# Decay sums of the first head pair on their own, masks made beside the first MLP layer, and a new order of the opening loads

## The chip, the cores and the metric

The kernel runs on one core of one Trainium2 chip. The metric is device time in microseconds (us). Times in the text count from the start of the profiled span unless they are durations. Engine names follow the profile: PE (matrix engine), DVE (vector), ACT (scalar), POOL (GpSimd) and SP (the engine that only issues transfers).

## The reference

The reference is an attention with a decay bias, whose output goes through a two-layer MLP with a hard-swish:

```python
batch, n_heads, seq, head_dim = (8, 8, 576, 64)
scores = q @ k.T / sqrt(64)                    # per head
cum = cumsum(max(s, 0))                        # per head, along the sequence
scores = where(causal, -1e9, scores + min(-(cum[i] - cum[j]), 0))
attn = softmax(scores); x = attn @ v           # (8, 8, 576, 64) -> (4608, 512)
h = x @ w_in                                   # w_in (512, 2048)
g = h * clip(h + 3, 0, 6) / 6
out = g @ w_out                                # w_out (2048, 512), out (4608, 512)
```

All inputs and the output are float32.

## The kernel before

**Units of work.** The 64 heads are taken in 32 pairs; pairs 4b to 4b+3 make up batch b. For a pair, q and k come in as 9 tiles of 128 rows (two heads of 576 rows), are cast to half size and turned, so that the head dimension lies on the partitions (`qT`, `kT`, both in `qkT`, three slots, pair p in slot p % 3). The decay enters as extra rows below the 64 rows of the head dimension: rows 64 to 67 carry the running sum, split in three half-size parts, and a row of ones. Rows 68 to 127 hold a mask by blocks of ten positions. Scores, exp on ACT, the product with v (`attend`), the division and the turn back into `xT` (`x_transpose`) follow. The MLP works on blocks of 512 tokens: `m1` is layer 1 (16 column groups, each four matmuls, an ACT and a DVE instruction), `m2` layer 2 (16 matmuls and a store for each 128 tokens).

**Order.** The program fixes the order on every engine by hand: each engine takes its instructions one after the other in the order in which the program issues them, with waits on semaphores between the engines. PE's order is fixed too. There are three stretches.

1. *Pairs 0 to 3 (batch 0).* There is no MLP work yet. `first_columns` gets the running sums of the first five pairs by four small matmuls of a scan with 0/1 matrices (`sums`), and writes them as columns 64 to 67 beside the cast q and k (`x0`), so that `turn_first` turns data and decay at once. `cast_first` casts q and k, `scores_half` computes half of a head's scores, with the causal mask added by a matmul of `ident` with `tri`. The mask rows of slot 0 are made on POOL by `select` at the very start (L154), the other slots' by DVE copies (`mask_rows`, L191).
2. *The passage to the MLP.* POOL issues the loads of `w_in` (L488) and `w_out` (L494), sets the ones of the decay rows (`aug_ones`, L194 and L195), and after DVE's `decay_scan` makes the rows (`decay_rows`, L147 to L151). PE meanwhile runs layer 1 of block 0. It turns the decay rows into columns (`decay_columns`, L263), which POOL puts in order (`decay_order`, L279 and L282). POOL casts pair 4 (L774, L301), and PE turns it (L780).
3. *Pairs 4 to 31*, woven with the MLP, and the rest of the MLP. Pairs 4 to 9 get their decay rows through memory (`store_aug`, `load_aug`), later ones as columns of `xb` with a transposing DMA.

**Queues.** Plain loads go through SP in the order of the program. The weights go through POOL's queue, since they are cast on the way. On SP, the store of the decay rows is followed by a `fence`, a small transfer that reads a row of the third quarter of `w_out_sb` and so waits for its load, and only then by the loads of pair 4. The lines of the passage read:

```python
    for c in range(4):
        load_w_out(c)
    aug_ones()
    ...
    decay_rows()
    store_aug(nc.sync)
    nc.sync.dma_start(out=fence_dram, in_=w_out_sb[0:1, 11, 0:32])
    load_pair(FIRST)
```

Of the kernel before, what the change touches and what calls it, by code (L numbers as in the profile page):

```python
# [9 lines left out]
F32 = mybir.dt.float32  # L10
# [6 lines left out]
def kernel(  # L17
# [48 lines left out]
    def pair_of_banks(b):  # L66
# [4 lines left out]
    NG = COLS * W2 // 64  # L71
    g = np.arange(NG)
    sel_np = g[:, None] == g[None, :]
    low_np = (g[:, None] < g[None, :]) & (g[:, None] // 9 == g[None, :] // 9)
    sums_dram = nc.inline_tensor(
        np.ascontiguousarray(
            np.stack([m[:, k::2] for k in range(2) for m in (sel_np, low_np)], axis=1)
        ).astype(np.float32),
        name="sums",
    )  # L80
# [28 lines left out]
    dec = cpool.tile([128, NTR, 4, NP], F16, tag="c_dec")  # L109
# [13 lines left out]
        "p (a t i c) -> p a t i c", a=COLS, t=NTR, i=2  # L123
# [3 lines left out]
    sums = work.tile([NG, 4, NG // 2], F32, tag="sums", bufs=1)  # L127
# [31 lines left out]
    def mask_view(sl, i):  # L159
# [4 lines left out]
    nc.vector.memset(x0[:, :, :, 0, D:D + 3], 1.0)  # L164
    nc.vector.memset(x0[:, :, :, 1, D + 3:D + 4], 1.0)
    both = [[0, 2], [1, SEQ]]
    select(
        mask_view(0, 1), both, 4 * GRAN, -GRAN, -16384.0,
        warm[64:128, 0:1].unsqueeze(1).to_broadcast([64, 2, SEQ]),
    )  # L170
    select(ident, [[1, 128]], 0, -1, 0.0, one[:, 0:1].to_broadcast([128, 128]))
    select(ident, [[-1, 128]], 0, 1, 0.0)

    def key_rows():
        nc.vector.memset(one[:, 1:2], 1.0)
        k_rows = mask_view(0, 0)
        select(
            k_rows, both, 4 * GRAN, -GRAN, 0.0,
            one[64:128, 1:2].unsqueeze(1).to_broadcast([64, 2, SEQ]),
        )  # L180
        select(k_rows, [[0, 2], [-1, SEQ]], -4 * GRAN + GRAN - 1, GRAN, 0.0)
        select(tri, [[1, 128]], 0, -1, -65504.0, warm[:, 0:128])
# [6 lines left out]

    def mask_rows(sl, i):  # L190
        nc.vector.tensor_copy(out=mask_view(sl, i), in_=mask_view(0, i))  # L191
# [81 lines left out]
    def decay_order():  # L273
        dv = dec_f.rearrange("p i (t a h) -> p t i a h", t=NTR, h=2)
        for r0, r1, j0, j1, h in (
            (0, 128, 0, 4, 0), (0, 64, 4, 5, 0), (64, 128, 4, 5, 1), (0, 128, 5, 9, 1)
        ):
            for i in range(3):
                nc.gpsimd.tensor_copy(  # L279
                    out=dec[r0:r1, j0:j1, i, :], in_=dv[r0:r1, j0:j1, i, :, h]  # L280
                )
        nc.gpsimd.tensor_scalar_mul(out=dec[:, :, 3, :], in0=dec[:, :, 0, :], scalar1=-1.0)  # L282

    def cast_columns(p):
        x = xb[:, p % 2]
        nc.gpsimd.tensor_copy(  # L286
            out=x.rearrange("p (i t) c -> p t i c", i=2)[:, :, :, 0:D], in_=qk_f.pop(p)
        )
        nc.gpsimd.tensor_copy(out=x[:, NTR:2 * NTR, D:D + 3], in_=dec[:, :, 0:3, p])
        nc.gpsimd.tensor_copy(out=x[:, 0:NTR, D + 3:D + 4], in_=dec[:, :, 3:4, p])  # L290
# [106 lines left out]
    def scores_half(hd, half):  # L397
        p, hh = hd // 2, hd % 2
        sl = p % NS
        off = hh * SEQ  # L400
        b, p0, parts, masks = HALVES[half]
        S = pair_of_banks(b)
        ops = []
        for kt, lo, hi, c in parts:
            ops.append((
                c, hi - lo, kT[:, sl, off + 128 * kt:off + 128 * (kt + 1)],
                qT[:, sl, off + lo:off + hi],
            ))
        for c, n in masks:
            ops.append((c, n, ident, tri[:, 0:n]))  # L410
        ops.sort(key=lambda o: o[0] // 512)
        for i, (c, n, lhsT, rhs) in enumerate(ops):
            bk = c // 512
            nc.tensor.matmul(  # L414
                out=S[:, c:c + n], lhsT=lhsT, rhs=rhs,
                start=(i == 0 or ops[i - 1][0] // 512 != bk),
                stop=(i == len(ops) - 1 or ops[i + 1][0] // 512 != bk),
            )
        n = max(c + n for c, n, _, _ in ops)
        nc.scalar.activation(  # L420
            out=Pm[:, hd % NS, p0:p0 + n], in_=S[:, 0:n], func=AF.Exp, scale=0.125, bias=0.0
        )
# [38 lines left out]
    def x_transpose(p):  # L461
        b, hp = p // (H // 2), p % (H // 2)
        xs = x_tiles.pop(p)
        if by_dma(p):

            nc.sync.dma_start(
                out=xT[:, hp, b * SEQ:b * SEQ + 640].rearrange("p (t c) -> p t c", c=128),
                in_=xs.rearrange("p t h d -> p (t h d)"),
                transpose=True,
            )  # L470
            return
        pX = f16(PS[:, 4 if p + 1 < FIRST else 2, :], 640) if p < FIRST else f16(bank("S"), 640)
        for qt in range(5):
            nc.tensor.matmul(  # L474
                out=pX[:, qt * 128:(qt + 1) * 128],
                lhsT=xs[:, qt, :, :],
                rhs=ident,
                is_transpose=True,
                start=(qt == 0),
                stop=(qt == 4),  # L480
            )
        nc.vector.tensor_copy(out=xT[:, hp, b * SEQ:(b + 1) * SEQ], in_=pX[:, 0:SEQ])  # L482
# [165 lines left out]
    def second_pair(p, fill):  # L648
# [27 lines left out]
        if first:  # L676
            transpose_group(p + 1, 0)
        if p + 3 < PTD:
            load_aug(p + 3, nc.sync)
# [66 lines left out]
    def first_columns():  # L746
# [6 lines left out]
        key_rows()  # L753
        cT = PS[:, 7, 0:NG // 2]
        for half in range(2):
            o = cT[64 * half:64 * half + 64, :]
            nc.tensor.matmul(
                out=o, lhsT=scan, rhs=sums[:, 2 * half, :], start=True, stop=False
            )
            nc.tensor.matmul(  # L760
                out=o, lhsT=scan[:, 63:64].to_broadcast([NG, 64]), rhs=sums[:, 2 * half + 1, :],
                start=False, stop=True,
            )
        c3 = cT.rearrange("p (a t) -> p a t", a=COLS)
        r3 = rest.rearrange("p (a t) -> p a t", a=COLS)
        hi, mid, lo = (x0[:, :, :, 1, D + j] for j in range(3))
        nc.vector.tensor_copy(out=hi, in_=c3)
        nc.scalar.activation(out=x0[:, :, :, 0, D + 3], in_=hi, func=AF.Copy, scale=-1.0)
# [4 lines left out]
    def cast_first(p, i, t0, t1, copy):  # L773
        copy(out=x0[:, p, t0:t1, i, 0:D], in_=qk_f[p][:, t0:t1, i, :])  # L774

    def turn_first(p, i, t0, t1, b, copy):
        pT = f16(pair_of_banks(b) if (t1 - t0) > 8 else PS[:, b, :], (t1 - t0) * 128)
        for t in range(t0, t1):
            c = (t - t0) * 128
            nc.tensor.matmul(  # L780
                out=pT[0:XW, c:c + 128], lhsT=x0[:, p, t, i, :], rhs=ident,
# [11 lines left out]
    A.dma_start(out=sums, in_=sums_dram.ap())  # L793
    load_part(0, 1, 0, 5, nc.sync)
    load_part(0, 0, 5, 9, nc.sync)
    load_part(0, 1, 5, 9, nc.sync)
    nc.scalar.preload_act_table_set("natural_log_exp_and_others")
    load_qk(1, nc.sync)
    load_v(0, nc.sync)
    load_qk(2, nc.sync)  # L800
    load_v(1, nc.sync)

    keep_warm(6)
    cast_first(0, 0, 0, 5, A.copy)
    cast_first(0, 1, 0, 5, A.copy)
    first_columns()
    keep_warm(2)
    turn_first(0, 0, 0, 5, 4, A.copy)
    turn_first(0, 1, 0, 5, 5, V.tensor_copy)
    cast_first(0, 0, 5, 9, G.tensor_copy)  # L810
    cast_first(0, 1, 5, 9, G.tensor_copy)
    for i in range(2):
        mask_rows(1, i)
    keep_warm(1)
    qk_f.pop(0)

    def cast_pair(p):
        for i in range(2):
            cast_first(p, i, 0, NTR, G.tensor_copy)
        qk_f.pop(p)  # L820

    for hd in range(2 * FIRST):
        p, odd = hd // 2, hd % 2
        scores_half(hd, 0)
        if hd == 0:
            turn_first(0, 0, 5, 9, 6, V.tensor_copy)
            turn_first(0, 1, 5, 9, 7, V.tensor_copy)
        if not odd:
            if p == 0:
                cast_pair(1)  # L830
                more_pads()
            if p == 2:
                for c in range(2):
                    load_w_in(c)
            cast_v(p)
            if p + 1 < FIRST:
                turn_first(p + 1, 0, 0, 9, 4, V.tensor_copy)
            if p == 2:
                for c in range(2, 4):
                    load_w_in(c)  # L840
            if p == 0:
                load_qk(3, nc.sync)
                load_v(2, nc.sync)
            if p == 1:
                load_v(3, nc.sync)
                nc.sync.dma_start(out=s_sb, in_=s.rearrange("b h t -> (b h) t"))
                load_columns()
        elif p + 1 < FIRST:
            turn_first(p + 1, 1, 0, 9, 4, V.tensor_copy)
            if p + 2 < FIRST:  # L850
                cast_pair(p + 2)
        scores_half(hd, 1)
        if hd > 0:
            attend(hd - 1)
        if hd == 1:
            for i in range(2):
                mask_rows(2, i)
        if odd and p > 0:
            x_transpose(p - 1)
# [3 lines left out]
    m1_0 = m1_tasks(0)  # L863
    attend(2 * FIRST - 1)
# [10 lines left out]
    decay_rows()  # L875
    store_aug(nc.sync)
    nc.sync.dma_start(out=fence_dram, in_=w_out_sb[0:1, 11, 0:32])
    load_pair(FIRST)
    for p in range(COLS, COLS + 2):
        load_pair(p)  # L880
        load_aug(p, nc.sync)
    run(m1_0[4:8])
# [9 lines left out]
    for i in range(2):  # L892
        copy_columns(i)
# [50 lines left out]
```

The softmax here doesn't subtract the row's maximum and nothing guards it: scores larger than these inputs give would overflow.

## Time and profile before

| | us |
|---|---|
| three runs | 360.22 to 360.40, median 360.33 |
| the profiled execution's own time | 359.87 |
| its span in the profile | 358.20 |
| PE busy | 349.6 (98%) |
| ACT busy | 208.8 (58%) |
| DVE busy | 182.9 (51%) |
| POOL busy | 153.3 (43%) |
| transfers, mean over the span | 165 GB/s |

The span is the stretch that the profiler covers, 1.67 us less than the execution's own time. Busy time counts what an engine's instructions took; waiting, branching and the issue of transfers are not in it. A row such as "22.19 2.17 POOL L494 ... x4" of the timeline gives start, length, engine, source line and how many instructions were merged; what stands in brackets is the idle time before it and what ended it. "DMA to landing" is the time from a transfer's issue to its completion.

### The profile page before, as it was taken

The numbers are of one execution on the slowest core, as the hardware profiler recorded it, in microseconds if no ns is written. First come the engines' busy times: TensorE is split into PE (matmuls) and PEld (weight loads), VectorE is DVE, ScalarE is ACT, GpSimd is POOL, SyncE is SP. The second block draws the span as 40 slices with busy tenths as digits, with TensorE's granted clock in tenths as the row PEclk, the third lists the DMA queues.
The fourth block names the chain that finished last, engine by engine and source line by source line (L and its number), as shares of the span: only waits on it lengthen the run. The fifth ranks groups of instructions, "written<-read, shape, count | busy, mean of one in ns | idle before, by whom it ended". The sixth has DMA issues, their size and how long they took to land.

```text
span 358.2 us, 7700 instructions
## 1 busy us (share of the span) xinstructions
PE 349.6 (98%) x2860; PEld 204.2 (57%) x2860; DVE 182.9 (51%) x314; ACT 208.8 (58%) x391; POOL 153.3 (43%) x378
## 2 busy tenths in 40 slices
PE   7999999999999999999999999999999999999996
PEld 3875557665655555555555555555555544544444
DVE  3758737766534553455435553545255536544531
ACT  3777437668847774677467755776477614533410
POOL 6694377765654444444444554555543200000000
PEclk9999999999999999999999999999999999999999
DMA  8999999999989999999998999999947110000012
GB/s 180 214 193 214 212 228 223 215 208 203 210 180 229 197 197 221 229 210 185 185 249 172 207 204 211 170 208 211 224 87 116 50 59 30 31 30 29 32 59 88
DMA packets 185312, 59.09 MB, mean 165 GB/s; under 512 B 177576, under 2 KB 180050, under 8 KB 185274
## 3 DMA queue, kind: packets, MB, share of 16 engines
q1 hardware_dynamic: 181681, 54.05, 72.0%
q0 software_dynamic: 2688, 4.19, 6.6%
q8 instruction: 22, 0.36, 0.4%
q10 hardware_dynamic: 905, 0.36, 0.4%
q14 instruction: 16, 0.13, 0.1%
HBM read 37.32 MB, written 9.53 MB: 131 GB/s over the span
## 4 chain that ended last, share of the span: by engine, by line
PE 84%; DVE 4%; ACT 3%; DMA 3%; POOL 3%; issue 1%; SPq 1%; POOLq 0%; ACTq 0%; DVEq 0%
PE PS L506 32%; PE PS L549 32%; PE PS L348 10%; PE PS L436 7%; DMA qkf<-in_k_dram 3%; DVE gT L517 2%; ACT trl L516 2%; DVE qkT L319 1%; ACT Pm L356 1%; PE PS L569 1%; PE PS L474 1%; PE PS L304 1%; POOL gT L774 1%; PE PS L414 1%; SPq L206 1%
## 5 line engine op out<-in xcount | busy, mean ns | idle before, releaser
L517 DVE SCALAR_TENSOR_TENSOR gT<-trl,PS 128x512 f16<-128x512 f32 x144 | 98.2, 687 | 103.0 <-ACT trl L516 102.9
L516 ACT ACTIVATE trl<-PS,bias 128x512 f32<-128x512 f32 x144 | 98.8, 692 | 78.3 <-PE PS L506 76.5
L506 PE MATMUL PS<-xT,w_in 128*128 128x512 f16 x576 | 143.2, 380 | 0.8 <-DVE gT L517 0.7
L549 PE MATMUL PS<-w_out_sb,gT 128*128 128x512 f16 x560 | 138.9, 379 | 0.0
L356 ACT ACTIVATE Pm<-PS 128x384 f16<-128x384 f32 x224 | 103.0, 507 | 45.7 <-PE PS L348 44.5
L361 POOL TENSOR_SCALAR_AFFINE_SELECT Pm<-Pm 128x256 f16<-128x256 f16 x224 | 68.4, 307 | 114.1 <-ACT Pm L356 106.3
L506 PEld LDWEIGHTS <-w_in 128*128 128x128 f16 x576 | 61.4, 114 | 45.7 <-issue 2.0
L549 PEld LDWEIGHTS <-gT 128*128 128x128 f16 x560 | 51.4, 98 | 48.2 <-issue 0.3
L348 PE MATMUL PS<-qkT 128*128 128x256 f16 x392 | 63.4, 261 | 0.8 <-DVE qkT L319 0.2
L348 PEld LDWEIGHTS <-qkT 128*128 128x128 f16 x392 | 36.0, 98 | 31.5 <-DVE qkT L319 2.4
L436 PEld LDWEIGHTS <-Pm 128*128 128x128 f16 x960 | 38.7, 97 | 11.0 <-ACT Pm L420 0.4
L436 PE MATMUL PS<-v_h,Pm 128*128 128x65 f16 x960 | 42.3, 194 | 0.6 <-ACT Pm L420 0.3
L558 DVE TENSOR_SCALAR osb<-PS 128x512 f32<-128x512 f32 x35 | 24.1, 688 | 33.9 <-PE PS L549 33.6
L448 DVE TENSOR_TENSOR xs<-PS,r 128x640 f16<-128x640 f32 x32 | 26.4, 824 | 1.1
L286 POOL CAST xb<-qkf 128x1152 f16<-128x1152 f32 x22 | 25.2, 1147 | 0.0
L301 POOL CAST v_h<-v_f 128x640 f16<-128x640 f32 x32 | 23.3, 728 | 0.8 <-DMA v_f<-in_v_dram 0.8
L420 ACT ACTIVATE Pm<-PS 128x896 f16<-128x896 f32 (+1 forms) x16 | 13.1, 836 | 4.5 <-PE PS L414 4.4
L319 DVE COPY qkT<-PS 64x640 f16<-64x640 f16 (+1 forms) x20 | 9.1, 454 | 8.9 <-PE PS L304 8.8
L446 DVE RECIPROCAL r<-PS 128x10 f32<-128x10 f32 x32 | 7.0, 217 | 9.2 <-PE PS L436 9.0
L414 PE MATMUL PS<-qkT 128*128 128x64 f16 (+4 forms) x48 | 9.4, 285 | 0.4 <-DVE qkT L786 0.2
L482 DVE COPY xT<-PS 128x576 f16<-128x576 f16 x14 | 6.4, 455 | 5.7 <-PE PS L474 4.5
L786 DVE COPY qkT<-PS 68x1152 f16<-68x1152 f16 (+2 forms) x13 | 7.2, 585 | 2.9 <-PE PS L780 1.9
(71 smaller groups left out, 119.0 us busy)
## 6 DMA issues: line engine op xcount, KB each, us to landing
out_dram<-osb SPq DMA_DIRECT2D x35, 256.0 KB, 2.7
qkf<-in_q_dram SPq DMA_DIRECT2D x31, 288.0 KB, 3.5
qkf<-in_k_dram SPq DMA_DIRECT2D x31, 288.0 KB, 4.2
v_f<-in_v_dram SPq DMA_DIRECT2D x64, 128.0 KB, 3.8
w_in<-in_moe_w_in_dram POOLq DMA_DIRECT2D x4, 512.0 KB, 9.8
w_out_sb<-in_moe_w_out_dram POOLq DMA_DIRECT2D x4, 512.0 KB, 16.2
v_f<-in_v_dram SPq DMA_DIRECT2D x32, 32.0 KB, 2.8
qkT<-xb SPq DMA_TRANSPOSE x22, 5.1
```

The source lines that it names most:

```text
L286: nc.gpsimd.tensor_copy(out=x.rearrange("p (i t) c -> p t i c", i=2)[:, :, :, 0:D], in_=qk_f.pop(p))
L301: nc.gpsimd.tensor_copy(out=v_h[:, sl, :, :, 0:D], in_=v_f[:, sl])
L348: nc.tensor.matmul(out=S[:, c:c + hi - lo], lhsT=kT[:, sl, off + 128 * kt:off + 128 * (kt + 1)], rhs=qT[:, sl, off + lo:off + hi], start=( ...
L356: nc.scalar.activation(out=P[:, p0:p0 + n], in_=S[:, 0:n], func=AF.Exp, scale=0.125, bias=0.0)
L361: nc.gpsimd.affine_select(out=view, in_=view, pattern=pattern, compare_op=ALU.is_ge, fill=0.0, base=0, channel_multiplier=-1,)
L436: nc.tensor.matmul(out=O[:, hh, qt * VW:qt * VW + D + 1], lhsT=P[:, c:c + 128], rhs=v_h[:, sl, hh, kt, 0:D + 1], start=(qt == 0), stop=(qt ...
L448: nc.vector.tensor_tensor(out=xs.rearrange("p t h d -> p h t d"), in0=Ov[:, :, :, 0:D], in1=r.to_broadcast([128, 2, 5, D]), op=ALU.mult,)
L506: nc.tensor.matmul(out=ph, lhsT=w_in_t[f // 4][:, kc, f % 4, :], rhs=xT[:, kc, n * 512:(n + 1) * 512], start=(kc == 0), stop=(kc == KC - 1),)
L516: nc.scalar.activation(out=trl, in_=ph, func=AF.Relu, bias=bias3[:, 0:1], scale=1.0)
L517: nc.vector.scalar_tensor_tensor(out=gT2[:, n % 2, f, :], in0=trl, scalar=6.0, in1=ph, op0=ALU.min, op1=ALU.mult)
L549: nc.tensor.matmul(out=po, lhsT=gT2[:, n % 2, f, t4 * 128:(t4 + 1) * 128], rhs=w_out_sb[:, f, :], start=(f == 0), stop=(f == NF - 1),)
L558: nc.vector.tensor_scalar_mul(out=osb, in0=po, scalar1=1.0 / 6.0)
```

## The change

The change reworks the first two stretches:

- The 0/1 matrices are in two parts: one for pair 0 alone (18 rows, 9 columns a matrix), one for pairs 1 to 4 (90 rows, 36 columns), each with its own load; `first_columns` runs twice, the second time after pair 0's scores have begun.
- The q and k columns of `x0` lie apart, and the sum's negative for q is made by ACT straight from the matmul's result.
- Scores of pairs 0 to 3 use rows 0 to 67 alone. The mask rows are made by `masks`, all on POOL, after `decay_rows`: three selects and four copies.
- Each v is loaded ahead of the next q and k; k's first three tiles of pair 0 are cast and turned on their own; turns, `attend` and `x_transpose` stand in another order; the loads of `w_in` stand between the casts of pairs 2 and 3.
- `more_pads` comes first on POOL. The columns `xaug` are loaded after pair 6's loads, and copied (`copy_columns`) during pairs 6 and 7.
- `decay_order` takes four copies; the sign of the fourth column is changed in `cast_columns`.
- The loop over `load_w_out` and `aug_ones()` stand twice, one after the other.

```diff
-    sums_dram = nc.inline_tensor(
...
+    sums_dram = [
+        nc.inline_tensor(np.ascontiguousarray(m).astype(np.float32), name=f"sums{i}")
+        for i, m in enumerate((sums_np[0:N0, :, 0:NTR], sums_np[:, :, NTR:]))
+    ]
...
-    select(
-        mask_view(0, 1), both, 4 * GRAN, -GRAN, -16384.0,
-        warm[64:128, 0:1].unsqueeze(1).to_broadcast([64, 2, SEQ]),
-    )
     select(ident, [[1, 128]], 0, -1, 0.0, one[:, 0:1].to_broadcast([128, 128]))
     select(ident, [[-1, 128]], 0, 1, 0.0)
-
-    def key_rows():
...
+    select(tri, [[1, 128]], 0, -1, -65504.0, warm[:, 0:128])
+
+    def masks():
+        both = [[0, 2], [1, SEQ]]
+        q_rows, k_rows = mask_view(0, 1), mask_view(0, 0)
+        select(
+            q_rows, both, 4 * GRAN, -GRAN, -16384.0,
+            warm[64:128, 0:1].unsqueeze(1).to_broadcast([64, 2, SEQ]),
+        )
         select(
             k_rows, both, 4 * GRAN, -GRAN, 0.0,
...
         select(k_rows, [[0, 2], [-1, SEQ]], -4 * GRAN + GRAN - 1, GRAN, 0.0)
-        select(tri, [[1, 128]], 0, -1, -65504.0, warm[:, 0:128])
+        for sl in range(1, NS):
+            for i in range(2):
+                nc.gpsimd.tensor_copy(out=mask_view(sl, i), in_=mask_view(0, i))
...
-            for i in range(3):
-                nc.gpsimd.tensor_copy(
-                    out=dec[r0:r1, j0:j1, i, :], in_=dv[r0:r1, j0:j1, i, :, h]
-                )
-        nc.gpsimd.tensor_scalar_mul(out=dec[:, :, 3, :], in0=dec[:, :, 0, :], scalar1=-1.0)
+            nc.gpsimd.tensor_copy(
+                out=dec[r0:r1, j0:j1, :, :], in_=dv[r0:r1, j0:j1, :, :, h]
+            )
...
-                c, hi - lo, kT[:, sl, off + 128 * kt:off + 128 * (kt + 1)],
-                qT[:, sl, off + lo:off + hi],
+                c, hi - lo, kT[0:XW, sl, off + 128 * kt:off + 128 * (kt + 1)],
+                qT[0:XW, sl, off + lo:off + hi],
...
+    more_pads()
+    keep_warm(5)
     cast_first(0, 0, 0, 5, A.copy)
-    cast_first(0, 1, 0, 5, A.copy)
-    first_columns()
-    keep_warm(2)
+    first_scan()
+    first_columns(0, 7)
+    cast_first(0, 1, 0, 3, V.tensor_copy)
+    keep_warm(1)
...
         scores_half(hd, 0)
         if hd == 0:
+            turn_first(0, 1, 3, 9, 7, V.tensor_copy)
             turn_first(0, 0, 5, 9, 6, V.tensor_copy)
...
+            first_columns(1, 5)
+            cast_v(0)
+            cast_pair(1)
+            load_v(3, nc.sync)
+            nc.sync.dma_start(out=s_sb, in_=s.rearrange("b h t -> (b h) t"))
         scores_half(hd, 1)
...
+        if hd == 2:
+            cast_v(2)
+            cast_pair(3)
+            load_w_in(1)
+        if hd == 3:
+            cast_v(3)
+            for c in range(2, 4):
+                load_w_in(c)
+    for c in range(4):
+        load_w_out(c)
+    aug_ones()
     for c in range(4):
         load_w_out(c)
     aug_ones()
     m1_0 = m1_tasks(0)
+    x_transpose(FIRST - 2)
     attend(2 * FIRST - 1)
...
     decay_rows()
+    masks()
     store_aug(nc.sync)
     nc.sync.dma_start(out=fence_dram, in_=w_out_sb[0:1, 11, 0:32])
     load_pair(FIRST)
     for p in range(COLS, COLS + 2):
         load_pair(p)
         load_aug(p, nc.sync)
+    load_columns()
...
-    for i in range(2):
-        copy_columns(i)
```

## The prediction

> **What bounds the kernel now.** I read the page's engine shares first, then TensorE's (PE's) waits and busy time by stretch, then the timeline around layer 1 of the first block, which the change touches.
>
> ```profile
> PE 349.6 (98%) x2860; PEld 204.2 (57%) x2860; DVE 182.9 (51%) x314; ACT 208.8 (58%) x391; POOL 153.3 (43%) x378
> ```
> ```profile
> 80.00:340.00 260.00, 258.83 (x1973) 147.27 (x1972) 126.81 (x204) 158.45 (x303) 100.22 (x266) 1.00 0.77 158
> ```
>
> PE is busy for 349.6 of 358.2 us, and from 80 to 340 us for 258.83 of 260. It takes its instructions in a fixed order, so a stall before 80 us finds about 1.2 us of idle time later to be made up in. The question is only what the change does to PE before 60 us. There the timeline has one narrow place:
>
> ```profile
> 22.19 2.17 POOL L494 DMA_DIRECT2D w_out_sb<-in_moe_w_out_dram x4
> 24.29 1.62 POOL L194 MEMSET aug<- 64x1728 f16 x1
> 25.76 0.66 POOL L195 MEMSET aug<- 64x576 f16 x1
> ```
> ```profile
> 30.13 0.66 POOL L147 CAST aug<-c 64x576 f16<-64x576 f32 x1 [3.71 <-DVE c L140]
> ...
> 32.94 1.27 POOL L151 TENSOR_TENSOR aug<-r,aug 64x576 f16<-64x576 f32 x1
> ```
> ```profile
> 35.03 0.65 PE L263 MATMUL PS<-idtri,aug 64*128 64x64 f16 x10
> ...
> 40.53 0.24 SPq L877 DMA_DIRECT2D fence<-w_out_sb  x1
> ...
> 42.24 3.62 PE L549 MATMUL PS<-w_out_sb,gT 128*128 128x512 f16 x16
> ...
> 45.10 1.27 POOL L774 CAST gT<-qkf 128x576 f16<-128x576 f32 x2
> 45.81 1.53 PE L780 MATMUL PS<-idtri,gT 128*68 128x128 f16 x18
> ```
>
> POOL issues the four w_out loads, sets the ones, and from 30.13 to 34.21 makes the decay rows that PE transposes at 35.03. Later POOL orders the decays and casts pair 4 (45.10), and PE turns it 0.04 us after the first cast ends (45.77). So POOL's order here is nearly PE's order. The third view is the w_out tile's and the w_in tile's time from issue to landing (least, median, most):
>
> ```profile
> DMA to landing us min/median/max: 13.3/16.2/19.4
> ```
> ```profile
> DMA to landing us min/median/max: 8.2/9.8/12.2
> ```
>
> The w_out issues stand at 22.2, 22.8, 23.3 and 23.8, so the chunks land at about 35.5, 37.9, 40.6 and 43.2; the last w_in lands at 20.8 + 12.2 = 33.0. One chunk lands every 2.5 us. SP's own wait list agrees:
>
> ```profile
> SPq L877 <- DMA w_out_sb<-in_moe_w_out_dram: 5.9, 1, 5.9
> ```
>
> **What the skill says.** (1) "DMA: Bandwidth & Descriptors", section "Two DMAs through the same engine are not ordered": one queue does not order a later transfer behind an earlier one, so the issuing engine must wait for the first one's semaphore. The trace agrees for a dependent transfer: SP stood 5.9 us for the fence. (2) The same page, "Issuing engines are not separate DMA queues": POOL's and SP's transfers share the same 16 engines. The trace agrees: DMA is busy throughout 20 to 40 us. (3) "GPSIMD Engine Reference", section 3.1: one-input bodies run at 1.03 cycles per element. At the page's 1.2 GHz that makes an estimated 0.99 us for 1,152 elements; the trace has 1.15 for a select of that size. (4) "TensorE: Matmul & The Clock Gate", Part 1: after an idle window of about 3.4 us the array runs at half rate until it has been busy that long. The opening warm-up matmuls are 0.43 us apart against 0.86 for four later, which agrees.
>
> **The change, part by part.**
>
> *The second w_out load.* The diff leaves the loop over load_w_out and aug_ones() standing twice. In the compiled order of the changed kernel, POOL's second set of four loads waits, chunk by chunk, for the landing of the same chunk of the first set (they write the same buffer). They stand ahead of the second aug_ones, the decay rows, the masks, the decay order and the cast of pair 4. So POOL, which waits in order, cannot begin the decay rows before the first set's last chunk has landed. In the trace of before that is 43.2. The changed kernel moves the xaug load (288 KB) behind it, 1.3 us at the 215 GB/s of this stretch, and SP's pair 4 loads, which shared the engines from 40.82, come later too (0 to 1.2 us; I take 0.7). The w_in and w_out issues keep their place within about 0.7 us and queue behind each other, so I take **41.2** for the last landing, 40 to 43.2 for the range.
>
> From there on POOL: issue of the last second-set chunk 0.58 (L494), 41.8; aug_ones again, 2.13 from start to end (24.29 to 26.42), 43.95; first decay row, 0.70 (L147), **44.65**, and PE may transpose it. PE arrives there near 35, so it stands some **9.6 us**. The four decay instructions end 4.08 after their start (30.13 to 34.21), at 48.0.
>
> *Masks beside layer 1.* Three selects of 64x1152 leave the front of POOL and come in here: 3 x 1.15 = 3.5. The copies to the two other slots, four on DVE before (L191), become POOL copies of 64x1152. The trace has none; the nearest are its f32 cast of 1,152 elements (L239, 1.14) and the select (1.15). I take 4 x 1.15 = 4.6, between 2.3 (were half-size types twice as fast) and 5.5 (DVE in the way: of the four copies at L191, beside POOL's casts, one took 1.13 us where 0.45 is usual). POOL is then at 56.1. Before, this was nothing on POOL's path here.
>
> *Decay order.* Twelve copies and one multiply (41.84 to 45.14, after two early ones) become four copies. A 128x128 copy is 0.29 and a 64x32 one 0.21; scaled by elements, 0.57 and 0.28, so 2 x 0.57 + 2 x 0.28 = 1.7: 57.9. The multiply by -1 goes into cast_columns, 9 elements for each of 22 pairs in place of a 0.22 copy; POOL is 43% busy, nothing is waiting on 0.1 us. The first cast of pair 4 (0.67) ends at **58.6**; in before at 45.77. PE's turn starts 58.6 - 45.81 = **12.8 us later**.
>
> *PE's own path to that point.* From the first decay transposes to the turn PE needs 45.86 - 35.03 = 10.8; from 44.65 that is 55.5, and up to 1.7 more (half of 3.4) for a cold array: 57.2. POOL is later by 1.4, so the clock's loss hides behind it.
>
> *SP.* The store of the decay rows waits for POOL at 48.0 (34.24 before), with the fence, all loads of pairs 4 to 6 and, now, xaug behind it. The fence needs the second set's third chunk: queued behind 41.2 at 2.5 us each it lands at 48.7. Pair 4's first load then starts at 49.1 and lands some 4.3 later (40.82 to 45.10 bounds it), 53.4, ahead of 57.9: hidden. The decay-row load for pair 5 waits for the masks (56.1) and holds pair 6 behind it; pair 6's load starts at 56.2, 2.4 before PE's turn, where before it came 3.1 after (48.92 against 45.81). So loads have gained room. PE's layer 2 (from about 53) needs the last chunk at 51.2: hidden.
>
> *The front.* The small first sum (18x36 against 90x180), k's three tiles cast on DVE, no selects ahead of the identity: first scores perhaps 1 us before 8.30. Four matmuls, one ACT and four DVE instructions are added for the other pairs' sums, under half a microsecond each. Scores over 68 rows stream the same columns: a 64-row transpose of 64 columns (L263) takes 191 ns and a 128-row matmul of 65 columns (L436) 194, so rows cost no time here, and I take nothing. Front gains end at PE's wait for the decay rows, which POOL and the transfers set: worth **0**. The new order of turns, attends and x_transposes lies ahead of the same wait: 0 too, with several microseconds of cover.
>
> *copy_columns* (DVE, 0.51 to 0.67 each) moves into pairs 6 and 7, where DVE has gaps of 0.66 (ahead of L319): 0, at most +1.1. Fresher loads may save part of the 0.9 us that PE idled between 46 and 56: down to -0.5. These I leave against each other.
>
> Sum against the profiled execution: 359.87 + 12.8 = 372.7 (span 358.2 + 12.8 = 371.0). The median of the runs is 360.33, 0.46 above that execution, so I forecast **373.1**; its own uncertainty is 371.6 to 374.8.
>
> **Rivals.**
> - *PE's path decides, not POOL's.* If the mask copies cost half, POOL is done by 56.3 and PE's cold 57.2 counts: +11.4, 371.7; with the landing at 40, 370.5. For it: the estimate of 1.15 rests on f32 and select rows. Against: selects in f16 cost the same as f32 casts. Chance 0.15.
> - *The second transfer decides.* If the second set lands late enough that pair 4 comes after 57.9 (its third chunk after about 53), each microsecond more counts: with 3.5 us a chunk about +15, 375.3. For it: sharing with SP's loads; against: SP is silent until 48. Chance 0.10.
> - *Faster.* If POOL's second loads did not hold it up, POOL would go decay rows 30.13 to 34.21, masks to 42.3, order to 44.0, cast at 44.0 against 45.10: about -1.1, 359.2. It needs the last landing before some 26 us, against 43.2 seen; only if the wait is not what the order shows. Chance 0.02; around zero 0.01.
> The rest, 0.72, is the forecast.
>
> **Numbers.** No change is within 0.2% (0.7 us), about what a measurement can tell here. Range 370.4 to 375.8: the rivals' ends below and above, with the late landing (43.2: +2.0, 375.1). Faster 0.02, same 0.01, slower 0.97.
>
> **What would show it.** Right: eight w_out issues on POOL, the last four apart by about 2.5 us and ending near 42; PE waiting for aug from POOL for 8 to 11 us; POOL going without a gap from there to the cast of pair 4 near 58; 80 us to the end shifted as a block. Wrong: second issues back to back; PE's first decay transposes before 40 us; or pair 4's cast waiting for a DMA.

## The result, and the profile after

| | before | after |
|---|---|---|
| median of four runs beside each other, us | 360.36 | 373.63 |
| lowest and highest | 360.22 to 360.40 | 373.32 to 374.36 |
| the profiled execution's own time | 359.87 | 374.36 |
| its span | 358.20 | 372.6 |

The changed kernel takes 1.0372 times as long, with a 95% interval of 1.0354 to 1.0390: 13.3 us more. The profiled execution of after is the slowest of its four, 0.73 us above their median, so times read from its trace stand about that much late.

The engine shares at the head of the page come first, then the table of two stretches, the late one moved by 14 us and a short one in the passage to the MLP. Its columns are the window, its length, busy time and count for PE, PEld, DVE, ACT and POOL, then the granted clock, the share of the transfer engines and GB/s.

```profile
PE 354.6 (95%) x2866; PEld 206.8 (56%) x2866; DVE 181.6 (49%) x314; ACT 208.0 (56%) x391; POOL 161.9 (43%) x379
```
```profile
94.00:354.00 260.00, 258.82 (x1974) 147.20 (x1973) 126.56 (x203) 158.94 (x305) 102.38 (x266) 1.00 0.75 157
40.00:44.00 4.00, 0.00 (x0) 0.00 (x0) 0.17 (x1) 0.00 (x0) 1.14 (x3) 0.59 1.06 213
```

From 94 us on PE is as full as it was from 80 on before (258.82 against 258.83 of 260): that part moved as a block. From 40 to 44 us PE does nothing at all, its clock falls to 0.59, and the transfer engines are full at 213 GB/s. POOL's timeline of this stretch says what goes on:

```profile
22.35 2.16 POOL L496 DMA_DIRECT2D w_out_sb<-in_moe_w_out_dram  x4
24.45 1.61 POOL L196 MEMSET aug<- 64x1728 f16 x1
25.93 0.65 POOL L197 MEMSET aug<- 64x576 f16 x1
35.98 0.54 POOL L496 DMA_DIRECT2D w_out_sb<-in_moe_w_out_dram  x1 [9.41 <-DMA w_out_sb<-in_moe_w_out_dram]
38.53 0.53 POOL L496 DMA_DIRECT2D w_out_sb<-in_moe_w_out_dram  x1 [2.01 <-DMA w_out_sb<-in_moe_w_out_dram]
40.97 0.53 POOL L496 DMA_DIRECT2D w_out_sb<-in_moe_w_out_dram  x1 [1.91 <-DMA w_out_sb<-in_moe_w_out_dram]
43.39 0.53 POOL L496 DMA_DIRECT2D w_out_sb<-in_moe_w_out_dram  x1 [1.90 <-DMA w_out_sb<-in_moe_w_out_dram]
43.91 1.56 POOL L196 MEMSET aug<- 64x1728 f16 x1
...
45.91 0.68 POOL L150 CAST aug<-c 64x576 f16<-64x576 f32 x1
...
53.62 4.42 POOL L187 COPY qkT<-qkT 64x1152 f16<-64x1152 f16 x4
58.10 1.60 POOL L280 COPY dec<-dec_f 128x384 f16<-128x384 f16 x4
59.65 1.27 POOL L781 CAST gT<-qkf 128x576 f16<-128x576 f32 x2
```

The first four issues of L496 follow each other without a pause. Each of the second four waits for a transfer into `w_out_sb`, and the first decay row (L150) comes 2.5 us after the last of them. The view of the `w_out_sb` tile gives the times from issue to landing of all eight loads; the last of the first set has the longest, 18.9 us from 23.95, and so lands at 42.85:

```profile
DMA to landing us min/median/max: 9.3/11.2/18.9
```

On PE this is the largest wait in the list, and in its timeline:

```profile
PE PS L265 <- POOL aug L150: 7.9, 1, 7.9
```
```profile
46.64 0.91 PE L265 MATMUL PS<-idtri,aug 64*128 64x64 f16 x10 [7.94 <-POOL aug L150]
...
55.80 3.62 PE L551 MATMUL PS<-w_out_sb,gT 128*128 128x512 f16 x16
60.36 1.53 PE L787 MATMUL PS<-idtri,gT 128*68 128x128 f16 x18 [0.95 <-POOL gT L781]
```

PE stands 7.9 us for the decay rows, then works 12.8 us on its own path (46.64 to 59.41; the first transposes at the lower clock, 0.91 instead of 0.65), and waits 0.95 us for the cast of pair 4. The turn of pair 4 starts at 60.36, 14.55 us after the 45.81 of before.

SP's queue issues the fence at 50.46, followed by the loads of pair 4:

```profile
50.46 0.38 SPq L895 DMA_DIRECT2D fence<-w_out_sb  x1
50.89 0.46 SPq L208 DMA_DIRECT2D qkf<-in_q_dram  x1
```

The loads of q and k in this stretch land 3.3 to 4.4 us after issue, so pair 4's are there at about 56, ahead of the cast at 59.65.

### The profile page after: what moved, and what is told of

It reads as the page before. It is cut to its first block, busy times and chain, and to the rows that moved or that the text cites. A ratio compares the mean times of both kernels' runs of the same rounds, so it can differ in the third digit from the quotient of the medians.

```text
span 372.6 us, 7714 instructions
## 1 busy us (share of the span) xinstructions
PE 354.6 (95%) x2866; PEld 206.8 (56%) x2866; DVE 181.6 (49%) x314; ACT 208.0 (56%) x391; POOL 161.9 (43%) x379
## 3 DMA queue, kind: packets, MB, share of 16 engines
q0 software_dynamic: 3264, 6.29, 9.3%
## 4 chain that ended last, share of the span: by engine, by line
PE 76%; DMA 8%; POOL 6%; DVE 3%; ACT 3%; SPq 2%; issue 1%; POOLq 0%; ACTq 0%
PE PS L551 30%; PE PS L508 27%; PE PS L350 10%; PE PS L438 6%; DMA w_out_sb<-in_moe_w_out_dram 5%; SPq L222 1%; DVE gT L519 1%; DVE qkT L321 1%; ACT trl L518 1%; ACT Pm L358 1%; POOL qkT L187 1%; DMA qkf<-in_k_dram 1%; PE PS L571 1%; POOL qkT L157 1%; PE PS L476 1%
## 5 line engine op out<-in xcount | busy, mean ns | idle before, releaser
L508 PE MATMUL PS<-xT,w_in 128*128 128x512 f16 x576 | 144.8, 383 | 0.8 <-DVE gT L519 0.7
L450 DVE TENSOR_TENSOR xs<-PS,r 128x640 f16<-128x640 f32 x32 | 26.4, 825 | 1.1
L793 DVE COPY qkT<-PS 68x1152 f16<-68x1152 f16 (+4 forms) x13 | 7.3, 586 | 9.2 <-PE PS L787 8.0
L416 PE MATMUL PS<-qkT 68*128 68x64 f16 (+4 forms) x48 | 10.4, 311 | 1.2 <-DVE qkT L793 1.1
L496 POOL DMA_DIRECT2D w_out_sb<-in_moe_w_out_dram x8 | 4.3, 550 | 15.2 <-DMA w_out_sb<-in_moe_w_out_dram 15.2
```

The costliest lines, as they stand in the source:

```text
L450: nc.vector.tensor_tensor(out=xs.rearrange("p t h d -> p h t d"), in0=Ov[:, :, :, 0:D], in1=r.to_broadcast([128, 2, 5, D]), op=ALU.mult,)
L508: nc.tensor.matmul(out=ph, lhsT=w_in_t[f // 4][:, kc, f % 4, :], rhs=xT[:, kc, n * 512:(n + 1) * 512], start=(kc == 0), stop=(kc == KC - 1),)
```

## The experiments

The theory: the second set of loads costs nearly everything, because POOL stands behind the first set's landing. The first rival: the rest of the change (masks on POOL, the new front) costs a good part. The second rival: the bytes of the second set cost the time, not POOL's wait. Runs e1_once to e4_ones_twice, e5_warm to e8_rows and e9_order were timed in three batches, each with the kernel before beside it; its medians there were 360.18, 360.08 and 359.93 us. A difference of a tenth or two between runs of different batches says nothing.

### The loads once (e1_once)

```diff
     for c in range(4):
         load_w_out(c)
     aug_ones()
-    for c in range(4):
-        load_w_out(c)
-    aug_ones()
```

> The changed kernel with the w_out loads and aug_ones issued once. Theory (POOL's wait for the first set holds up the decay rows): PE finds the rows ready and does not stall at the decay transposes. PE came to them at 38.7 in the changed kernel against 35.03 before, so pair 4's turn starts at 38.7 + 10.8 = 49.5, 3.7 later than before; POOL's own chain (rows from 33.7, four instructions 4.1, masks 8.0, order 1.6, cast 0.7) ends at 48.1 and is not the bound. About 364.0 us, 362.5 to 365. Rival (the masks on POOL or the new front cost the 13 us): 370 or more.

Measured: 363.85 us (363.53 to 364.45), ratio 1.0102 [1.0081, 1.0123]. That is 9.8 us less than the changed kernel, and 3.7 us more than the kernel before in the same batch. PE's timeline no longer shows a wait at the decay rows nor at the cast of pair 4:

```profile
30.23 1.46 PE L508 MATMUL PS<-xT,w_in 128*128 128x512 f16 x6
...
39.29 0.65 PE L265 MATMUL PS<-idtri,aug 64*128 64x64 f16 x10
...
49.96 1.17 PE L787 MATMUL PS<-idtri,gT 128*68 128x128 f16 x18
```

POOL has the decay rows from 34.40 on, ends the masks at 46.54, and starts casting pair 4 at 48.15. PE comes at 49.96, so masks, order and casts on POOL are hidden here. The 4 us by which the turn is late are there already when layer 1 begins, at 30.23 here and at 25.97 in the kernel before:

```profile
25.97 1.48 PE L506 MATMUL PS<-xT,w_in 128*128 128x512 f16 x6
```

### The kernel before with the loads twice (e2_before_twice)

```diff
     aug_ones()
+    for c in range(4):
+        load_w_out(c)
+    aug_ones()
     m1_0 = m1_tasks(0)
```

> The kernel before with one edit: the w_out loads and aug_ones issued a second time. Theory: last landing of the first set near 43.2, issue about 1.1 after it, aug_ones 2.1, first decay row 0.7: PE goes on at 47 instead of 35.03 and is cold for a while; the cast of pair 4 follows 10.1 later plus up to 1.7, so +12 to +14: 372.4 to 374.4 us, about 373.5. Rival (the wait costs little, masks and front do): 362 to 365.

Measured: 373.28 us (372.64 to 373.64), ratio 1.0360 [1.0339, 1.0381]. The second set alone costs the kernel before 13.1 us; with the rest of the change on top it is 373.63, only 0.35 more (their intervals overlap), though the rest alone costs 3.7. Costs do not add where one wait swallows another. PE's wait list and timeline of this kernel show it:

```profile
PE PS L263 <- POOL aug L147: 11.9, 1, 11.9
```
```profile
46.58 0.91 PE L263 MATMUL PS<-idtri,aug 64*128 64x64 f16 x10 [11.92 <-POOL aug L147]
```

PE comes 4 us earlier than in the changed kernel (it waits 11.9 us, not 7.9), and goes on at the same moment, 46.58 against 46.64. In both kernels the last load of the first set lands at about 42.8, and that sets the moment, though their fronts differ.

### The same bytes into another buffer (e3_aside)

The second set writes columns of `xT` that are not in use yet, and so does not wait for the first set.

```diff
-    def load_w_out(c):
+    def load_w_out(c, aside=False):
...
-            out=w_out_sb[:, c * 4:(c + 1) * 4, :],
+            out=xT[:, :, 2304 + 512 * c:2816 + 512 * c] if aside
+            else w_out_sb[:, c * 4:(c + 1) * 4, :],
...
     for c in range(4):
-        load_w_out(c)
+        load_w_out(c, aside=True)
     aug_ones()
```

> The changed kernel, but the second set of w_out loads goes to columns of xT that are not used until much later, so it moves the same bytes and does not wait for the first set (each waits only for the w_in chunk of the same number, landed by about 33). Theory (waiting, not bytes): POOL issues the last one near 33.6, aug_ones to 36, first decay row 36.7, before PE comes at 38.7; cast of pair 4 near 50.5. 364 to 366.5 us. Rival (the bytes cost the time: pair 4's loads and layer 2 share the engines with the second set): 370 or more.

Measured: 371.62 us (369.70 to 373.41), ratio 1.0306 [1.0254, 1.0358]. The theory's expectation failed. Taking the wait away frees about 2 us, where 7 to 10 were expected; as the four runs spread over 3.7 us, the 2 is uncertain by about as much. POOL issues the second set at 26.4 to 33.4 and PE transposes the decay rows at 38.97, as foreseen. But the profile, here first the wait lists of PE and POOL and then the timeline, shows a new place:

```profile
PE PS L788 <- POOL gT L782: 7.2, 2, 4.0
```
```profile
POOL gT L782 <- DMA qkf<-in_q_dram: 5.1, 2, 3.1
```
```profile
41.11 0.40 SPq L208 DMA_DIRECT2D qkf<-in_q_dram  x1
...
42.86 9.76 SPq L222 DMA_DIRECT2D v_f<-in_v_dram  x2
...
53.06 0.66 POOL L782 CAST gT<-qkf 128x576 f16<-128x576 f32 x1 [3.09 <-DMA qkf<-in_q_dram]
...
56.71 0.67 POOL L782 CAST gT<-qkf 128x576 f16<-128x576 f32 x1 [2.99 <-DMA qkf<-in_k_dram]
```

Pair 4's q is issued at 41.11, about as early as in the kernel before (40.82), and is cast only at 53.06, when it has come; k takes 15.1 us from issue to landing, where the loads of this stretch took 3.3 to 4.4 us in the changed kernel. The transfer engines are full from 40 to 56 us (195 to 228 GB/s), and the second set is in front or beside: by their times from issue to landing its four chunks come at about 46.1, 49.4, 52.8 and 56.1, and k right after them, at 56.7. SP is held up too: two loads of v take it 9.76 us to issue, where two took 1.77 us in the changed kernel. The Trainium skill, "DMA: Bandwidth & Descriptors", section "Issuing engines are not separate DMA queues", says that transfers run on the same 16 engines and interleave, whichever engine issued them; the trace agrees, with 12 and 15 us instead of 4.

So the second set costs time in two ways: with the wait and the bytes 9.8 us, with the bytes alone about 7.8 (371.62 less 363.85). What the wait would cost without the bytes was not measured. In the changed kernel the two lie over each other: until 50 us, while POOL waits, SP has nothing issued, so most of the bytes flow when nobody else needs the engines. Only when both are gone, in e1_once, does the time come back.

One thing besides the wait differs in e3_aside: the columns of `xT` lie in shorter pieces, so POOL's queue moved 4,800 packets where it moved 3,264 in the changed kernel. How much of the 7.8 us comes from the smaller packets was not separated.

### aug_ones twice, the loads once (e4_ones_twice)

```diff
     aug_ones()
-    for c in range(4):
-        load_w_out(c)
     aug_ones()
```

> The changed kernel with the w_out loads once and aug_ones twice. Theory: the second memsets lie in POOL's idle time before the decay scan is done (26.6 to 33.7), so the time is that of the run with everything once, within 0.5 us. Rival (the memsets are on the path): 2 us more than that.

Measured: 363.53 us (one run), within the runs of e1_once (363.53 to 364.45). The second memsets, about 2 us of POOL (43.91 to 45.91 in after), cost nothing here: in e1_once POOL stands 7.5 us for DVE's scan ahead of the decay rows anyway.

### Three more warm-up matmuls (e5_warm)

What are the remaining 3.7 us? PE's timeline of the opening of e1_once shows matmuls of 512 columns at two prices:

```profile
6.82 0.61 PE L416 MATMUL PS<-qkT 68*128 68x512 f16 x1
...
10.37 0.63 PE L416 MATMUL PS<-qkT 68*128 68x512 f16 x1
...
16.20 0.39 PE L416 MATMUL PS<-qkT 68*128 68x512 f16 x1 [0.38 <-DVE qkT L793]
```

I read the array's rate from these durations: 0.61 to 0.63 us is half rate and 0.38 to 0.39 full rate. The profile's column of the granted clock does not tell them apart, it shows 1.00 throughout the opening. By its durations the array is at half rate until about 15 us (in the trace of after until about 13.3); in the kernel before its 512-column matmul is at 0.61 at 8.30 and at 0.39 at 10.69. On top of e1_once:

```diff
-    keep_warm(5)
+    keep_warm(6)
...
-    keep_warm(1)
+    keep_warm(2)
     turn_first(0, 0, 0, 5, 4, A.copy)
+    keep_warm(1)
     turn_first(0, 1, 0, 3, 5, V.tensor_copy)
```

> Everything of the changed kernel with the w_out loads and aug_ones once (363.9 us), and three more warm-up matmuls in the opening: one more at the start, one more after pair 0's sums, one between the turns of q and k. In the run with everything once, PE's 68x512 score matmul still takes 0.63 at 10.4 us, and the half-rate turns (0.107 apart) go on to about 13 us; the kernel before is at full rate from about 9. Theory (a cold array is most of the 3.6 us that remain over before): full rate 2 to 4 us sooner, half of it gained less some 0.4 for the added matmuls: 362 to 363.3 us. Rival (the order of turns and its waits on DVE's copies is the cost): 363.9 or a little more.

Measured: 361.53 us (361.43 to 362.79), ratio 1.0050 [1.0031, 1.0069]. Three added matmuls save 2.3 us. The first 512-column score matmul is now at full rate, and pair 4's turn starts at 47.59, 2.4 earlier:

```profile
7.38 0.39 PE L416 MATMUL PS<-qkT 68*128 68x512 f16 x1
```

### Turns between the score halves (e6_turns), and both (e7_both)

In the new order PE turns a pair's tiles and then needs DVE's copy of them at once: `L416` waits three times for it, 1.1 us together, in e1_once and in after. e6_turns puts the turns from pair 2 on (`hd > 1`) between the two halves of a head's scores, so that the copy lies beside PE's work; e7_both has this and the warm-up matmuls.

```diff
+        if hd > 1:
+            turn_next(p + 1, hd % 2)
         scores_half(hd, 1)
...
         elif odd:
             attend(hd - 1)
-            turn_next(p + 1, 1)
...
-            turn_next(p + 1, 0)
```

> Everything once, and from pair 1 on the turn of the next pair's q or k stands between the two score halves, as in the kernel before, not after them. In the run with everything once PE waits three times about 0.4 for DVE's copy of the turned k, 1.1 in all, and loads weights 0.5 late as often. Theory (the order is the cost): 362.3 to 363 us. Rival (cold array): no more than 0.3 faster than 363.9.

> Both edits together: three more warm-up matmuls, and the turns between the score halves. If both causes hold and add up: 361 to 362.5 us. If the front is then ahead of the first w_in chunk or of pair 4's loads (fence at 41.5, first cast possible near 46), no less than 360.3.

Measured: e6_turns 363.03 us (362.67 to 363.04), ratio 1.0084 [1.0067, 1.0101], 0.8 less than e1_once; the runs of the two do not overlap, the intervals of their ratios do. In its PE wait list one of the three waits is left, and there is a new one of the same length at `L476`:

```profile
PE PS L476 <- DVE qkT L793: 0.4, 1, 0.4
PE PS L416 <- DVE qkT L793: 0.4, 1, 0.4
```

e7_both: 360.52 us (360.27 to 362.64), ratio 1.0017 [1.0007, 1.0027]. The two savings add up: 2.3 and 0.8 were found one by one, 3.3 together. Of the 3.7 us, 0.4 are left.

### Scores over all rows (e8_rows)

On top of e1_once the scores of batch 0 take all 128 rows again; the lower rows hold zeros from three memsets, one on POOL and two on DVE.

```diff
-                c, hi - lo, kT[0:XW, sl, off + 128 * kt:off + 128 * (kt + 1)],
-                qT[0:XW, sl, off + lo:off + hi],
+                c, hi - lo, kT[:, sl, off + 128 * kt:off + 128 * (kt + 1)],
+                qT[:, sl, off + lo:off + hi],
...
```

> Everything once, and the scores of pairs 0 to 3 over all 128 rows as before, with the lower rows set to zero by three memsets in idle time of POOL and DVE. Theory of the prediction (rows are free): 363.9 within 0.5 us. Rival (68 of 128 rows load the array less, and it comes to full rate later): 1 to 2 us faster, the array at full rate before 11 us.

Measured: 362.89 us (362.67 to 363.09), ratio 1.0085 [1.0065, 1.0105], 1.0 less than e1_once, with no overlap of the runs, though the intervals of the two ratios overlap. PE's timeline has the second head's 512-column matmul at full rate:

```profile
6.93 0.61 PE L416 MATMUL PS<-qkT 128*128 128x512 f16 x1
...
10.35 0.38 PE L416 MATMUL PS<-qkT 128*128 128x512 f16 x1
```

A matmul over 68 rows is no faster than one over 128 (0.61 and 0.61 cold, 0.39 and 0.38 warm), but with 128 rows the array is at full rate some 5 us earlier than in e1_once. Of that only 1.0 us reaches the end: PE then meets waits for ACT and DVE (0.35 at 11.35, 0.57 at 13.50) that the slow matmuls had covered. One trace of each kernel would not be enough, because the onset varies: the kernel before and e2_before_twice have the same opening, and their matmuls become fast by 10.1 and by 7.0 us. But five kernels have this opening with 68 rows (after, e1_once, e3_aside, e4_ones_twice and e6_turns). In each of their traces the nine turns that begin between 12.0 and 12.4 us still take 1.16 or 1.17 us together, where e8_rows has 0.67 from 11.79 on, and full rate begins between about 13.3 and 15 us. So the traces speak for a later onset with fewer rows; with 128 rows in this opening there is only one. How the chip counts activity they do not show.

### One more order (e9_order)

On top of e7_both, to beat the kernel before: pair 1's q is turned between the halves of head 1, and `x_transpose` stands behind the `attend` that followed it.

```diff
+        if hd == 1:
+            turn_next(1, 0)
         scores_half(hd, 1)
         if hd == 1:
-            turn_next(1, 0)
             attend(0)
...
-                x_transpose(p - 2)
                 attend(hd - 1)
+                x_transpose(p - 2)
```

> The changed kernel with the loads of w_out and aug_ones once, three more warm-up matmuls and the turns between the score halves, and two more moves: the turn of pair 1's q goes between the score halves of head 1, and each x_transpose of pairs 0 and 1 goes behind the attend that followed it. Theory (what is left of the loss against the kernel before is PE's waits for DVE's copies in the first four pairs): three waits of about 0.4 us each (the q-turn's copy ahead of the k-turn, the k-turn's copy ahead of pair 1's scores, the copy ahead of the x_transpose) shrink to one or none, layer 1 begins near 26.0 instead of 26.7, and the time is 359.6 to 360.1, equal to or a little under the kernel before. Rival (PE is in step with DVE's and ACT's own work there, so a wait taken away at one place comes back at the next): 360.4 to 360.7, layer 1 still near 26.7.

Measured: 360.64 us (360.24 to 364.01), ratio 1.0029 [1.0015, 1.0042]; its interval overlaps that of e7_both. Layer 1 begins at 26.31, 0.4 before e7_both, between the two expectations. Part of the waits came back at the next place, as the rival said:

```profile
PE PS L787 <- DVE xT L484: 0.7, 1, 0.7
```

No version with the new front beats the kernel before.

## Why the prediction was right, and where its steps were off

The forecast was 373.1 us, the measurement 373.63: right in direction, size and cause. That the two lie within 0.5 us is in part luck. In the trace of after PE's turn is 14.55 us later and not 12.8, an error of 1.75; but this execution lies 0.73 us above the median of its four, and the forecast had added 0.46 to get from the profiled execution of before to the median. The two take most of the error away. The steps in order:

| step | predicted | in the trace of after |
|---|---|---|
| last chunk of the first set lands | 41.2 (40 to 43.2) | 42.85 (issued 23.95, 18.9 to landing) |
| first decay row ready, PE goes on | 44.65 | 46.64 |
| PE's wait there | 9.6 (sign of being right: 8 to 11) | 7.9 |
| decay rows end | 48.0 | 50.0 |
| four mask copies | 4.6 | 4.42 |
| decay order | 1.7 | 1.60 |
| first cast of pair 4 ends | 58.6 | 60.3 |
| POOL behind PE's own path | 1.4 | 0.95 |
| shift of PE's turn | 12.8 | 14.55 in the profiled run |

- **The second load.** Right: eight issues, the last four one landing apart, and everything on POOL behind them. e1_once shows that no stall remains without it.
- **The landing.** The mis-sized term. I took 2.0 us off the 43.2 of before, because 288 KB of `xaug` move away and SP's loads come later. The last landing moved by only 0.35, to 42.85. In e2_before_twice, where `xaug` is still loaded early, the last landing is at 42.8 too and PE goes on at the same time, 46.58. Moving those bytes away is worth nothing measurable here.
- **From landing to issue.** Not in the sum. By the view's own numbers the last chunk lands at 42.85 and the next issue starts at 43.39, 0.54 later. The two errors together are 2.2 of the 2.0 us by which PE went on late; the shorter issue and memsets give the rest back.
- **Masks, order, cast.** Right within 0.3 us together, in the trace of after. That they would decide over PE's own path held by 0.95 us. They add little: e2_before_twice has no masks there and its turn starts at 59.55, 0.8 us before after's 60.36.
- **The cold array after the stall.** PE's path from the decay transposes to the turn took 12.8 us, not the 10.8 of before: 2.0 where I allowed up to 1.7; the granted clock was 0.50 from 46 to 50 us and 0.88 from 50 to 54. It hid behind POOL, as said, with 0.95 us to spare.
- **SP.** The fence at 50.46 for 48.7, pair 4's load at 50.89 for 49.1: late by the same 1.8, hidden as said. The loads' cover is thinner than the text made it: e3_aside shows that the second set's bytes alone bring back nearly the whole loss.
- **The front.** "Worth 0" came out right for the sum and wrong for the reason. I expected the front to gain about 1 us and the stall to hide it. First scores did start earlier (6.61 against 8.30), but layer 1 began 3.6 us later (29.57 against 25.97). This is why PE waited 7.9 and not 9.6 us. Without the stall the front costs 3.7 us, of which 2.3 went with three warm-up matmuls and 0.8 to 1.0 with the order of the turns. "Rows cost no time" was right for one matmul; for the kernel, e8_rows with all rows was 1.0 us faster.
- **Rivals.** PE's path deciding missed by 0.95 us. The second transfer deciding did not come: pair 4's data lay ready nearly 4 us before its cast. Faster did not come; its premise, POOL not held up, was built in e3_aside, and there the bytes took the place of the wait, which that rival had left out.

The last 0.4 us between e7_both and the kernel before was not pursued beyond e9_order.

## What to carry to other kernels

Here a load issued again into a buffer that was still being filled held POOL, which issued it, for 15.2 us in four waits; in such a case look for what stands behind the load on that engine, not at the load. When a stall is to be removed, ask what its time hides: here taking away the wait and the bytes together gave 9.8 us, the wait alone 2.0. A part called free because it lies ahead of a wait is free only while the wait is there, so measure it once with the wait gone.

## What the runs showed of the hardware that I had not expected

- **The array can stay at half rate for much longer than PE's busy time suggests.** In e1_once PE is busy in all of these two stretches, and its matmuls are at half rate:

```profile
7.00:10.00 3.00, 3.00 (x26) 1.00 1.26 255
10.00:13.00 3.00, 3.00 (x25) 1.00 1.25 252
```

The Trainium skill's "TensorE: Matmul & The Clock Gate", Part 1, speaks of some 3.4 us of sustained activity, watched in a window that runs freely. From that figure I estimate that two whole windows, 6.8 us, are the longest that a busy array should have to wait. In the five traces with 68-row scores PE is busy by its records for 98% or more of every microsecond from 6 to 13 us, and full rate comes only between about 13.3 and 15 us, 7 to 9 us after that stretch begins. With 128 rows (e8_rows) it came at about 10.2 us, after some 4. So busy records are not the activity that the page means, or the rule is not the whole of it; the number of rows is the likeliest cause of the difference, and not a proven one.

- **Loads took three to four times as long behind queued weights.** q and k loads of 288 KB, 3.3 to 4.4 us in the passage of the changed kernel, took 12 us (to the cast of q) and 15 us (k) in e3_aside, beside four queued chunks of 512 KB.
- **A waiting issue started about half a microsecond after the landing.** On POOL in the changed kernel this is 42.85 to 43.39 for the last of the four, and between 0.5 and 0.6 us for the other three too.
